# Narrower first weight loads, another order of k, q and v, and one attention block a group later, in a fused retention and gated feed-forward kernel

## The chip, the cores and the metric

The kernel runs on one core of a Trainium2 chip. The metric is the device time in microseconds (us) of one execution. A core has a matrix engine (PE, with its weight loads listed as PEld), a vector engine (DVE), a scalar engine for activations and copies (ACT), a general engine (POOL) and a synchronisation engine (SP). POOL, SP and ACT also issue transfers to the 16 DMA engines of the core. Each engine runs its own list of instructions in order; semaphores let one list wait for another. The matrix engine writes to PSUM, of which this kernel has eight banks: one reserved for the state sums (`z`) and seven that are handed round for everything else (they all carry the name `ff` in the profile).

## The reference

Two stages follow each other: a recurrent linear attention with a decay per head, and a feed-forward layer with a sigmoid gate.

```python
# q, k, v: (4 batches, 8 heads, 768 tokens, 64); gamma[h] = 1 - 2 ** (-5 - h)
for t in range(S):
    state = gamma * state + einsum('bhd,bhe->bhde', k[:, :, t], v[:, :, t])
    y[:, :, t] = 1 / sqrt(D) * einsum('bhd,bhde->bhe', q[:, :, t], state)
x = y.transpose(0, 2, 1, 3).reshape(3072, 512)
gate = 1 / (1 + exp(-(x @ w_gate)))         # w_gate, w_val: 512 x 1536
out = (gate * (x @ w_val)) @ w_out          # w_out: 1536 x 512
```

## The kernel before

**Attention.** The 768 tokens of each batch are cut into six chunks of 128, numbered 0 to 23 over the four batches. Within a chunk the recurrence becomes matrix products: scores of k and q (`scores`), a causal mask on DVE (`masks`), masked scores times v (`intra`), and q times the state that the earlier chunks left (`inter`). The decay is folded into v (`scale_v`, table `tabv`) and taken out again in the output (`y_out`, tables `taby`). `state` makes a chunk's share of the state, `state_sum` adds it up on DVE, `casts` turns the sum on ACT into a bf16 block matrix `zbd` for the next chunk's `inter`. `block(done, new)` does all this for two finished and two new chunks in one go: `inter` of the done, `scores` of the new, `intra` of the done, `state` of the new, then the vector work. Chunks 0 to 3 take a special path at the start (`..._run`). The transposes of k and q are made by the matrix engine for chunks 4 to 7 (`step_t`) and by DMA transposes that SP issues from chunk 8 on (`xbar`, line 169).

**Feed-forward.** The 3072 tokens are six tiles of 512 (four chunks each). `up(t, n1)` makes one row block of 128 of the 1536 hidden features: four matmuls with `wg`, four with `wv`, a sigmoid on ACT (`gs`), a product on DVE (`hT`). `up_columns` does several row blocks for 256 tokens in one pair of banks. `down` makes the output with `wo`, ACT copies it out and SP stores it.

**Order.** Everything is written out by hand. In the loop over the tiles `t` each `up` and each half of a `down` is a group; `plan[t]` (lines 536 to 548) names the attention steps that follow group `i`, and `ahead` (lines 557 to 563) the transfers that go before it. In tile 1 groups 0 to 7 are `up(1, 0..7)` for the first 256 tokens, groups 8 to 11 are the `up_columns` of the other 256, groups from 12 on are full `up`s. So `(4, block, 6, 8)` puts the block that ends chunks 6, 7 and starts 8, 9 behind `up(1, 4)`.

**Loads.** All loads that change type, and nearly all others, are issued by POOL in the order in which they are written: `load_run` for k, q, v of the first chunks, `load_gate_val(s)` for 256 columns of `wg` and `wv` (lines 83 to 87), `load_out` for `wo`, `load_chunk` for k, q and v of one chunk. A load takes one of eight semaphores in turn, so POOL waits before each load until the one eight loads earlier has landed. `load_behind(10)` waits for the transposes of chunk 8 before it loads chunks 10 and 11.

Of the kernel before, what the change touches and what calls it, by code (L numbers as in the profile page):

```python
# [17 lines left out]
def kernel(  # L18
# [10 lines left out]
    nc = tc.nc  # L29
# [29 lines left out]
    def load_v(g):  # L59
        vf[g] = ld.tile([C, H, D], F32, tag="vf", name="vf", bufs=6)  # L60
        nc.gpsimd.dma_start(out=vf[g], in_=src(v, g))  # L61

    def load_kq(g):
        kn[g] = ld.tile([C, H, D], BF16, tag="kn", name="kn")
        qn[g] = ld.tile([C, H, D], BF16, tag="qn", name="qn")
        nc.gpsimd.dma_start(out=kn[g], in_=src(k, g))  # L66
        nc.gpsimd.dma_start(out=qn[g], in_=src(q, g))  # L67

    def load_chunk(g):
        load_kq(g)  # L70
        load_v(g)
# [8 lines left out]
    wv = wpool.tile([128, KT, D_FF], BF16, name="wv")  # L80
    wo = wpool.tile([128, NFF, D_MODEL], BF16, name="wo")

    def load_gate_val(s):
        cols = slice(s * 256, (s + 1) * 256)
        for dst, w in ((wg, moe_w_gate), (wv, moe_w_val)):
            nc.gpsimd.dma_start(out=dst[:, :, cols],
                                in_=w.rearrange("(kk p) n -> p kk n", p=128)[:, :, cols])

    def load_out(s):
        nc.gpsimd.dma_start(out=wo[:, s * 3:(s + 1) * 3, :],  # L90
                            in_=moe_w_out.rearrange("(n p) d -> p n d", p=128)[:, s * 3:(s + 1) * 3, :])
# [60 lines left out]
    def bank(shape, dt=F32):  # L152
        return pf.tile(shape, dt, tag="ff", name="ff")
# [85 lines left out]
    def x_cols(t, kk, lo, hi):  # L239
        if hi - lo == 512:  # L240
            return xT[t][:, :, kk, :]
        half = lo // 256
        return xT[t][:, half, kk, lo - half * 256:hi - half * 256]
# [11 lines left out]
    def runs(t):  # L255
        return t.rearrange("x h (j d) -> x h j d", j=2)
# [19 lines left out]
    def scale_run(a, eng):  # L276
        vsr[a] = const.tile([128, H, 2, D], BF16, name=f"vsr{a}")
        eng.tensor_tensor(vsr[a], runs(vr[a]), tabr[:, a].unsqueeze(3).to_broadcast([128, H, 2, D]), op=ALU.mult)  # L278
# [20 lines left out]
    def inter_run(g, first=True):  # L299
        a, c = divmod(g, 2)  # L300
        if first:
            y[g] = bank([128, NP, C])
        if g > 0:
            for p in range(NP):
                nc.tensor.matmul(y[g][:, p, :], zbd[g - 1][:, p, :], qT[a][:, p, :, c * D:(c + 1) * D],
                                 start=(first and p == 0), stop=not first, skip_group_check=True)
# [72 lines left out]
    def up(t, n1, lo=0, hi=512, between=None):  # L379
        if t not in hT:  # L380
            hT[t] = ffn.tile([128, NFF, 512], BF16, tag="hT", name="hT", bufs=2)
        ps = []
        for w in (wg, wv):
            u = bank([128, 512])
            for kk in range(KT):
                nc.tensor.matmul(u[:, lo:hi], w[:, kk, n1 * 128:(n1 + 1) * 128], x_cols(t, kk, lo, hi),  # L386
                                 start=(kk == 0), stop=(kk == KT - 1))
            ps.append(u)
        if between:
            between()  # L390
        gs = ffn.tile([128, 512], F32, tag="gs", name="gs")
        nc.scalar.activation(gs[:, lo:hi], ps[0][:, lo:hi], AX.Sigmoid)  # L392
        nc.vector.tensor_tensor(hT[t][:, n1, lo:hi], gs[:, lo:hi], ps[1][:, lo:hi], op=ALU.mult)  # L393

    def up_columns(t, n1s, lo, hi, rows=1):
        if t not in hT:
            hT[t] = ffn.tile([128, NFF, 512], BF16, tag="hT", name="hT", bufs=2)
        n = hi - lo
        us = [bank([128, 512]), bank([128, 512])]
        for row in range(rows):  # L400
            for w, u in zip((wg, wv), us):
                for i, n1 in enumerate(n1s):
                    for kk in range(row * KT // rows, (row + 1) * KT // rows):
                        nc.tensor.matmul(u[:, i * n:(i + 1) * n], w[:, kk, n1 * 128:(n1 + 1) * 128],  # L404
                                         x_cols(t, kk, lo, hi), start=(kk == 0 and (rows == 1 or i == 0)),
                                         stop=(kk == KT - 1), skip_group_check=rows > 1)
        ps = [u[:, :len(n1s) * n] for u in us]
        gs = ffn.tile([128, 512], F32, tag="gs", name="gs")
        g = gs[:, :len(n1s) * n]
        nc.scalar.activation(g, ps[0], AX.Sigmoid)  # L410
        nc.vector.tensor_tensor(hT[t][:, n1s[0]:n1s[-1] + 1, lo:hi], g.rearrange("p (i n) -> p i n", n=n),  # L411
                                ps[1].rearrange("p (i n) -> p i n", n=n), op=ALU.mult)
# [18 lines left out]
    def keep_on(n, u):  # L431
        for _ in range(n):
            nc.tensor.matmul(u, ident, ident4, start=True, stop=True)  # L433
# [24 lines left out]
    for i in range(2):  # L458
        half = maskr[i * D:(i + 1) * D]
        nc.gpsimd.affine_select(half, half, pattern=[[-1, 2], [1, 2], [2, D]], base=0, channel_multiplier=-2,  # L460
                                compare_op=ALU.is_ge, fill=0.0)
    maskr2 = maskr.rearrange("x j i p -> x (j i p)").unsqueeze(1).to_broadcast([128, 2, 4 * D])
    load_gate_val(0)
    load_gate_val(1)
    load_gate_val(2)
    scale_run(1, nc.gpsimd)
    warm = bank([128, 4, 128])
    keep_on(9, warm)
    kT[0], qT[0], kT[1], qT[1] = (new_run_T() for _ in range(4))
# [22 lines left out]
    masks_run(1, 0)  # L492
    masks_run(1, 1)
    keep_on(2, warm)
    up_columns(0, range(0, 2), 0, 256)
    inter_run(2)
    state_run(1)
    sum_run(2)
# [11 lines left out]
    extend_taby(5)  # L510
    for s in range(4):
        load_out(s)
    for g in range(4, 8):
        load_chunk(g)
    y[3] = bank([128, NP, C])
    intra_run(1, [3])
    y_out_run(2)
# [15 lines left out]
    def downs(t):  # L533
# [2 lines left out]
    plan = {  # L536
        0: [(9, step_t, 4), (10, step_t, 5), (11, block, None, 4), (12, step_t, 6), (13, casts, 4), (13, step_t, 7),
            (14, block, 4, 6), (15, scale_v, 8)],
        1: [(0, casts, 6), (2, scale_v, 9), (4, block, 6, 8), (6, casts, 8), (10, scale_v, 10), (11, scale_v, 11),
            (12, block, 8, 10), (14, casts, 10), (16, scale_v, 12), (17, scale_v, 13), (20, block, 10, 12),  # L540
            (22, casts, 12)],
        2: [(3, scale_v, 14), (4, scale_v, 15), (6, block, 12, 14), (8, casts, 14), (11, scale_v, 16),
# [69 lines left out]
```

## Time and profile before

| what | value |
|---|---|
| median of 4 runs | 231.28 us (230.95 to 231.86) |
| the profiled execution: its time, its span | 231.15 us, 229.4 us |
| PE, PEld busy | 219.3 us (96%), 119.0 us (52%) |
| DVE, ACT, POOL busy | 117.8 us, 87.1 us, 78.5 us |
| mean granted clock of PE | 0.998 |
| POOL's DMA queue (q0) | 55440 packets, 16.78 MB |
| one 256-column load of `wg` or `wv` | 256 KB as written, 7.2 or 7.8 us from issue to landing (median) |

The span is the stretch from the first to the last instruction that the profiler recorded. The profiled execution's own time has 1.75 us more than its span. Sizes of loads and rates in GB/s count the bytes that are written: a load that turns f32 into bf16 reads twice as much.

### The profile page before, as it was taken

To read this page: it belongs to the slowest core of one execution; us is meant where nothing else is said; L and a number is where in the kernel's file an instruction comes from. 1 tells how busy PE (TensorE), PEld (TensorE's weight loads), DVE (VectorE), ACT (ScalarE), POOL (GpSimd) and SP (SyncE) were. 2 spreads that over 40 slices of the span, in tenths; PEclk is the share of its full clock that TensorE was granted. 3 is DMA by queue.
4 is the path that set the end of the run, shared out by engine and by line. 5 is a ranking of instruction groups with operands and counts; after the bars stand their busy time and mean duration, and the time that the engine had idled before them with its cause. 6 is when DMAs were issued, how large, how long until landed. Compare 5 with 4: busy or idle time off the path is not lost.

```text
span 229.4 us, 4519 instructions
## 1 busy us (share of the span) xinstructions
PE 219.3 (96%) x1803; PEld 119.0 (52%) x1815; DVE 117.8 (51%) x224; ACT 87.1 (38%) x162; POOL 78.5 (34%) x106
## 2 busy tenths in 40 slices
PE   4989999999799999999999999999999999999994
PEld 1458544567687445445445445455445454444443
DVE  5687333459776927367626267637267520243301
ACT  5785332554362421632521532622432512433221
POOL 7899956840906353081630090620000000000000
PEclk9999999999999999999999999999999999999999
DMA  8999999999996999499892399892410012100022
GB/s 135 217 196 197 198 206 195 180 245 202 154 173 36 176 137 228 120 127 162 61 202 96 91 130 138 90 197 83 108 39 3 0 49 91 46 0 0 4 91 91
DMA packets 77653, 28.08 MB, mean 122 GB/s; under 512 B 64192, under 2 KB 73280, under 8 KB 77632
## 3 DMA queue, kind: packets, MB, share of 16 engines
q0 software_dynamic: 55440, 16.78, 66.0%
q1 hardware_dynamic: 22048, 10.95, 22.9%
q8 instruction: 14, 0.23, 0.4%
q10 hardware_dynamic: 144, 0.07, 0.1%
q14 instruction: 7, 0.06, 0.1%
HBM read 28.31 MB, written 6.29 MB: 151 GB/s over the span
## 4 chain that ended last, share of the span: by engine, by line
PE 84%; DMA 10%; POOL 2%; issue 1%; DVE 1%; SPq 1%; DVEq 0%
PE ff L386 47%; PE ff L422 23%; PE ff L404 5%; DMA kn<-in_k_dram 4%; DMA wv<-in_moe_w_val_dram 3%; PE ff L232 2%; DMA qkX<-qn 2%; DMA vr<-in_v_dram 2%; PE ff L183 2%; PE ff L195 1%; PE ff L441 1%; PE z L201 1%; DVE vsr L278 1%; SPq L169 1%; PE ff L162 0%
## 5 line engine op out<-in xcount | busy, mean ns | idle before, releaser
L393 DVE TENSOR_TENSOR hT<-gs,ff 128x512 bf16<-128x512 f32 (+1 forms) x70 | 44.7, 647 | 59.2 <-PE ff L386 53.4
L386 PE MATMUL ff<-xT,wg 128*128 128x512 bf16 (+1 forms) x280 | 67.7, 364 | 0.2 <-DVE hT L393 0.2
L386 PE MATMUL ff<-xT,wv 128*128 128x512 bf16 (+1 forms) x280 | 67.6, 364 | 0.1
L392 ACT ACTIVATE gs<-ff 128x512 f32<-128x512 f32 (+1 forms) x70 | 39.4, 567 | 68.2 <-PE ff L386 62.2
L422 PE MATMUL ff<-wo,hT 128*128 128x512 bf16 x264 | 61.1, 379 | 0.9 <-issue 0.5
L386 PEld LDWEIGHTS <-wv 128*128 128x128 bf16 x280 | 27.3, 98 | 29.3 <-DMA wv<-in_moe_w_val_dram 0.3
L422 PEld LDWEIGHTS <-hT 128*128 128x128 bf16 x276 | 26.4, 98 | 30.5
L386 PEld LDWEIGHTS <-wg 128*128 128x128 bf16 x280 | 26.8, 98 | 28.3 <-issue 0.4
L427 ACT COPY ob<-ff 128x512 f32<-128x512 f32 x23 | 13.5, 585 | 49.1 <-PE ff L422 39.0
L250 DVE TENSOR_TENSOR xT<-ff,taby 128x512 bf16<-128x512 f32 x20 | 12.9, 685 | 24.0 <-PE ff L232 24.0
L553 POOL COPY gate<-qkX 1x1 bf16<-1x1 bf16 x7 | 1.2, 177 | 58.7 <-DMA qkX<-qn 58.7
L66 POOL DMA_DIRECT2D kn<-in_k_dram x20 | 17.8, 892 | 7.7 <-DMA qkX<-kn 2.9
L207 ACT CAST zbd<-za 64x256 bf16<-64x256 f32 x38 | 15.3, 403 | 10.0 <-DVE za L219 4.8
L61 POOL DMA_DIRECT2D vf<-in_v_dram x20 | 18.3, 917 | 1.6 <-DMA wo<-in_moe_w_out_dram 1.0
L67 POOL DMA_DIRECT2D qn<-in_q_dram x20 | 18.0, 898 | 2.0 <-DMA wo<-in_moe_w_out_dram 1.6
L174 DVE TENSOR_TENSOR vs<-vf,tabv 128x512 bf16<-128x512 f32 x20 | 13.5, 685 | 5.6 <-DMA vf<-in_v_dram 5.6
L188 DVE TENSOR_TENSOR stA<-ff,causal 128x512 bf16<-128x512 f32 x20 | 13.6, 679 | 0.0
L189 DVE TENSOR_TENSOR stB<-ff,causal 128x512 bf16<-128x512 f32 x20 | 13.6, 679 | 0.0
L433 PE MATMUL ff<-ident 128*128 128x512 bf16 x15 | 5.8, 527 | 3.0 <-POOL ident masks.py:199 3.0
L404 PE MATMUL ff<-xT,wg 128*128 128x256 bf16 x56 | 7.3, 273 | 0.7 <-DMA wg<-in_moe_w_gate_dram 0.7
L404 PE MATMUL ff<-xT,wv 128*128 128x256 bf16 x56 | 7.3, 273 | 0.3 <-DMA wv<-in_moe_w_val_dram 0.3
L411 DVE TENSOR_TENSOR hT<-gs,ff 128x512 bf16<-128x512 f32 x7 | 4.7, 687 | 3.9 <-PE ff L404 3.8
(86 smaller groups left out, 150.1 us busy)
## 6 DMA issues: line engine op xcount, KB each, us to landing
out_dram<-ob SPq DMA_DIRECT2D x23, 256.0 KB, 2.2
vf<-in_v_dram POOLq DMA_DIRECT2D x20, 256.0 KB, 5.7
kn<-in_k_dram POOLq DMA_DIRECT2D x20, 128.0 KB, 5.5
qn<-in_q_dram POOLq DMA_DIRECT2D x20, 128.0 KB, 5.7
wg<-in_moe_w_gate_dram POOLq DMA_DIRECT2D x6, 256.0 KB, 7.2
wv<-in_moe_w_val_dram POOLq DMA_DIRECT2D x6, 256.0 KB, 7.8
wo<-in_moe_w_out_dram POOLq DMA_DIRECT2D x4, 384.0 KB, 9.6
vr<-in_v_dram SPq DMA_DIRECT2D x1, 512.0 KB, 4.4
```

The lines of the kernel that those rows point to most:

```text
L61: nc.gpsimd.dma_start(out=vf[g], in_=src(v, g))
L66: nc.gpsimd.dma_start(out=kn[g], in_=src(k, g))
L67: nc.gpsimd.dma_start(out=qn[g], in_=src(q, g))
L174: nc.vector.tensor_tensor(vs[g], vf[g], tabv[:, g % NCH, :].unsqueeze(2).to_broadcast([C, H, D]), op=ALU.mult)
L188: nc.vector.tensor_tensor(stA[g], sc[g][0], causal4, op=ALU.mult)
L189: nc.vector.tensor_tensor(stB[g], sc[g][1], causal4, op=ALU.mult)
L207: nc.scalar.copy(zbd[g % 4][half, :, half], z[half])
L386: nc.tensor.matmul(u[:, lo:hi], w[:, kk, n1 * 128:(n1 + 1) * 128], x_cols(t, kk, lo, hi), start=(kk == 0), stop=(kk == KT - 1))
L392: nc.scalar.activation(gs[:, lo:hi], ps[0][:, lo:hi], AX.Sigmoid)
L393: nc.vector.tensor_tensor(hT[t][:, n1, lo:hi], gs[:, lo:hi], ps[1][:, lo:hi], op=ALU.mult)
L404: nc.tensor.matmul(u[:, i * n:(i + 1) * n], w[:, kk, n1 * 128:(n1 + 1) * 128], x_cols(t, kk, lo, hi), start=(kk == 0 and (rows == 1 or i = ...
L422: nc.tensor.matmul(o, hT[t][:, n1, sm * 128:(sm + 1) * 128], wo[:, n1, :], start=(n1 == 0), stop=(n1 == NFF - 1))
```

## The change

1. `load_gate_val` gets a width. The first 256 columns of `wg` and `wv` are loaded in four pieces of 128 columns (gate 0, value 0, gate 1, value 1) in place of two of 256. The work on the first 256 tokens of tile 0 follows the pieces: `up(0, 0)` and `up(0, 1)` in place of one `up_columns` for both row blocks. POOL's `scale_run(1)` keeps six loads before it; the loads of the third block of columns come behind it.
2. Chunks 6 and 7: k and q of both are loaded first, then v of both.
3. In tile 1 `block(6, 8)` comes behind group 5 in place of 4; `casts(6)` behind group 2 in place of 0, `scale_v(9)` behind 3 in place of 2, `casts(8)` behind 9 in place of 6.

```diff
-    def load_gate_val(s):
-        cols = slice(s * 256, (s + 1) * 256)
+    def load_gate_val(s, width=256):
+        cols = slice(s * width, (s + 1) * width)
...
-    load_gate_val(0)
+    load_gate_val(0, 128)
+    load_gate_val(1, 128)
     load_gate_val(1)
+    scale_run(1, nc.gpsimd)
     load_gate_val(2)
-    scale_run(1, nc.gpsimd)
...
-    up_columns(0, range(0, 2), 0, 256)
+    up(0, 0, 0, 256)
+    up(0, 1, 0, 256)
...
-    for g in range(4, 8):
-        load_chunk(g)
+    load_chunk(4)
+    load_chunk(5)
+    for load in (load_kq, load_v):
+        load(6)
+        load(7)
...
-        1: [(0, casts, 6), (2, scale_v, 9), (4, block, 6, 8), (6, casts, 8), (10, scale_v, 10), (11, scale_v, 11),
+        1: [(2, casts, 6), (3, scale_v, 9), (5, block, 6, 8), (9, casts, 8), (10, scale_v, 10), (11, scale_v, 11),
```

## The prediction

> **What bounds the kernel now.** I read the page's busy rows first, then the list of whom PE waits for, then the chain around the longest of these waits, then PE's and ACT's timeline there, and last the rates of the load queue by stretch.
>
> ```profile
> span 229.4 us, 4519 instructions
> PE 219.3 (96%) x1803; PEld 119.0 (52%) x1815; DVE 117.8 (51%) x224; ACT 87.1 (38%) x162; POOL 78.5 (34%) x106
> DMA  8999999999996999499892399892410012100022
> ```
> ```profile
> PE ff L183 <- DMA qkX<-qn: 1.1, 1, 1.1
> PE ff L404 <- DMA wg<-in_moe_w_gate_dram: 0.7, 1, 0.7
> ...
> PE ff L404 <- DMA wv<-in_moe_w_val_dram: 0.3, 1, 0.3
> PE ff L386 <- DVE hT L393: 0.2, 1, 0.2
> PE ff L162 <- DMA qn<-in_q_dram: 0.2, 1, 0.2
> ```
> ```profile
> 45.67 8.07 DMA kn<-in_k_dram
> ...
> 53.77 1.19 SPq L169
> ...
> 55.00 4.72 DMA qkX<-qn
> 59.72 0.14 issue
> 59.86 0.40 PE ff L183 x8
> ```
> ```profile
> 56.88 0.60 PE L386 MATMUL ff<-xT,wg 128*128 128x256 bf16 x4 [0.19 <-DVE hT L393]
> 57.58 0.60 PE L386 MATMUL ff<-xT,wv 128*128 128x256 bf16 x4
> 58.01 0.39 PE L195 MATMUL ff<-qkT,zbd 128*128 128x128 bf16 x4
> 58.33 0.40 PE L183 MATMUL ff<-qkX 64*128 64x128 bf16 x8
> 59.86 0.40 PE L183 MATMUL ff<-qkX 64*128 64x128 bf16 x8 [1.13 <-DMA qkX<-qn]
> ```
> ```profile
> 55.47 1.65 ACT L207 CAST zbd<-za 64x256 bf16<-64x256 f32 x4 [1.36 <-DVE za L217]
> ```
> ```profile
> 6.00:9.00 3.00, 3.00 (x70) 1.58 (x69) 1.36 (x4) 1.82 (x4) 2.24 (x6) 1.00 1.75 174
> 14.00:27.00 13.00, 11.99 (x152) 8.64 (x152) 8.30 (x15) 7.04 (x14) 12.93 (x17) 1.00 1.45 197
> ```
>
> PE is busy for 96% of the span at full clock (the 1.00 before the last two figures of the last fence's rows is the granted clock, then come DMA share and GB/s written). Past 61.0 us PE's waits are only two "issue" gaps of 0.16 us and 0.1 us for DVE at 61.9, so a change pays only through the waits of the second fence. The last of them in time, 1.13 us at 59.86, decides: there PE needs the transposed k and q of chunk 9, and by the chain this moment is set by transfers alone (k of chunk 9 issued at 45.67, landed 8.1 us later; the transpose of q issued at 55.00, landed at 59.72). The busy share of the DMA engines is 9 tenths from the first slices to about 55 us: the whole stretch is one full load queue. So whatever PE gains or loses before 58 us is swallowed by this wait, and the end of the kernel is: landing of chunk 9's transposes, plus the PE work that then remains.
>
> **The change part by part.**
>
> *The weight pieces.* In the last fence the final number of a row is GB/s written. A 256-column load (256 KB, 512 B per row) takes 262144 B / 197 GB/s = 1.33 us of the queue. No row shows a 128-column weight piece (128 KB, 256 B per row), but the first k and q loads write the same 256 B out of 512 B: 131072 B / 174 GB/s = 0.75 us (between 6 and 7 us the rate was 183 GB/s, which makes 0.72). Four pieces in place of two loads: 4 x 0.75 - 2 x 1.33 = +0.34 us; with 0.72 it is +0.22. I take 0.28. The bounds: at the wide loads' 197 GB/s the pieces cost nothing (0); if a piece took the queue as long as a wide load, +2.66. The value lies by the rows with the same piece size, at the low end.
>
> On this stage: before, PE started on the first gate columns at 14.72, the value columns at 16.04 and ended at 16.92 (0.44 us for each four matmuls). After, gate 0 can be there at about 14.1, but PE also needs `y_out_run(1)`, which ends at 14.32. Value 1 is the fourth piece and lands 4 x 0.75 - 2 x 1.33 = 0.34 later than the second load did, so PE ends at 16.04 + 0.34 + 0.44 = 16.82, 0.1 earlier. The next value columns (needed by `up(0, 2)`, 18.69 before, straight off the queue) come 0.3 later, so PE is 0.3 late from there: the 0.7 and 0.3 us waits are moved, not removed. Two sigmoids and two products in place of one each cost 2 x 0.38 - 0.60 = 0.16 us on ACT and 2 x 0.41 - 0.69 = 0.13 on DVE, both under the waits for weights. POOL issues two loads more, 2 x 0.76 = 1.5 us; `scale_run(1)` keeps its place, `extend_taby(3)` ends about 1.6 us later, at 18.0, and its reader starts at 19.6. POOL's later issues stay at least 2 us ahead of the queue, until the wait for the load eight places earlier sets their pace as before.
>
> *The order of chunks 6 and 7.* The same bytes; q of 7 comes one v load earlier (256 KB at the 233 GB/s of the stretch from 45 to 49 us, 1.1 us), which ends PE's wait at 48.28 (0.32 us with the matmuls that were held up). v of 6 lands about 2.3 us later, near 48.5; DVE scales it and v of 7 by 50.5, and the state matmuls need them at 51.4. What is late next: PE is at chunk 7's scores 0.2 us before ACT has copied its transposes. Worth 0.15 us net, in front of the wait: nothing at the end.
>
> *The block one group later.* `up(1, 5)` (0.875 us: eight matmuls between 61.01 and 61.885) moves in front of the block, that is in front of the wait, and no longer stands behind it: -0.875. For this PE has to reach chunk 9's scores before they land. In front of the block PE now loses 0.36 us at 56.88 and 0.26 at 57.58, because ACT does the casts (1.65 us) ahead of the sigmoids of groups 1 to 4. With the casts behind group 2 the sigmoids of 0 to 2 go first, banks come free in time and both gaps close (DVE's first product, held by the masks to 56.4 before and 56.6 after, frees its banks for group 5 at 57.6). PE starts tile 1 at 53.2 (53.03 before, 0.15 for chunk 7) and is at chunk 9's scores after six groups, `inter(7)` and chunk 8's scores: 53.2 + 6 x 0.875 + 2 x 0.22 = 58.9. They land at 59.72 + 0.28 = 60.0. So the wait stays, at about 1.1 us. The casts end at 57.6; `inter(7)` needs the first of them at 58.4. `scale_v(9)` ends near 59.0, its state matmuls come at 61.2. `casts(8)` now holds ACT from 66.6 to 68.25 and one sigmoid by 0.5 us, under PE work of seven banks; their reader, `block(8, 10)`, comes at 72. On SP and POOL nothing else is moved past: the transposes of chunks 10 and 11 hang on the same queue, 0.28 us later, landed at 71.0 before, needed at 73.2 before and 72.6 after.
>
> *Sum.* -0.875 + 0.28 = -0.60 us against the profiled execution's 231.15: 230.55, a span of 228.8. The median of the runs is 0.13 above that execution, so 230.68 for a median. Measurements of this kernel tell about 0.3% (0.69 us) from no change; the forecast of -0.26% lies just inside.
>
> *A rule against the trace.* The Trainium skill ("DMA: Bandwidth & Descriptors", section "Why small descriptors are slow (HBM only)") gives each packet about 3 cycles on top of one per 32 B. By it a 256 B piece takes 11 cycles and a 512 B one 19, an estimate of 0.77 us for the piece, +0.42 on the queue and -0.45 at the end, not -0.60. The same page's "Specifications" has DMA engines read before they write below 512 B, which speaks against narrow pieces; the rows at 174 to 183 GB/s against 197 show a loss of 7 to 12%.
>
> **The rivals.**
>
> *The delay does not reach chunk 9.* If the pieces move at the wide rate, or the 8.1 us that a load spends in the queue hold slack, the landing stays at 59.72 and the gain is the whole group: 231.28 - 0.875 = 230.4. For: the bytes written fall from 233 GB/s between 45 and 49 us to 221 between 50 and 54. Against: the engines' share stays at 9 tenths there.
>
> *The group is not won.* The wait grows by as much as PE is earlier, or DVE's products (DVE is busy without a gap from 51.4 to 56.8) take over as the wait behind the block: 231.3. This needs +0.875 on the queue, a piece of 0.88 us or 149 GB/s, below any row of 256 B pieces.
>
> *Slower: a piece costs the queue what a wide load costs.* A price per packet, not per byte: 512 packets either way. Then chunk 9 lands 2.66 us later and the end moves by -0.875 + 2.66 = +1.8: 233.1. It becomes slower than before from a piece of 0.88 us on, and slower by 0.3% from 1.06. For: the packet count of the four pieces is double that of the two loads, and their rows lie 6 KB apart, where k's lie together. Against: the queue passed 197 GB/s / 512 B = 385 packets of a wide load in a microsecond, but 174 GB/s / 256 B = 680 of the first k and q.
>
> **How the numbers follow.** Main case 0.58, 230.68; its own range 230.4 to 230.95 (+0.22 to +0.34 on the queue, and 0.2 for the scatter of a median); it falls to 0.24 faster, 0.34 same. No delay at chunk 9: 0.20, of which 0.18 faster, 0.02 same. Group not won: 0.08, 0.07 same and 0.01 slower. Per-packet price: 0.14, slower. Together faster 0.42, same 0.43, slower 0.15. The low end is the full group with 0.3 us of scatter below, 230.1; the high end is the case of no gain with 0.3 above, 231.6. That leaves out the per-packet case and a few hundredths.
>
> **What would show it.** Right: PE's wait for the transposed q still there and 1.0 to 1.3 us long, near 60.1; `up(1, 5)` in front of it with no gaps at group 4; the wait for gate columns below 0.4 us and a longer one for value columns at `up(0, 2)`; rates of 170 to 185 GB/s in the first 3 us of weights. Wrong: the transposes of chunk 9 landing before 59.7 or after 60.4, PE coming to them later than they land, or a new wait past 62 us.

## The result

The changed kernel takes 231.81 us (median of 44 runs, 230.97 to 234.14) where the kernel before, on the same chip, takes 231.27 (63 runs, 230.56 to 233.34): a ratio of 1.0035, 95% interval 1.0023 to 1.0047. It is slower by 0.54 us; forecast was 0.60 us less, in a range of 230.1 to 231.6. In 13 of the 44 executions the mean granted clock was 0.993; half the clock for some 3.4 us, as two traces further down show it, would make this mean. The median of the other 31 is 231.64, still +0.37. Among the later experiments one execution of `changed_third` took 384.29 us at a mean clock of 0.66 and one of `ahead_columns` 261.02 us at 0.855; the medians and ratios given for these two leave them out.

The profiled execution of the changed kernel took 231.12 us, the third fastest of the 44, and its span is that of the kernel before. So it shows why the forecast gain is missing; the 0.69 us more that the median execution took are not in it. First its page, the same rows as were shown of before:

```profile
span 229.4 us, 4525 instructions
PE 219.2 (96%) x1803; PEld 119.1 (52%) x1815; DVE 117.9 (51%) x225; ACT 87.6 (38%) x163; POOL 80.1 (35%) x108
DMA  7999999999998999999792399992420012100022
```

Then whom PE waited for, in us in total, times, longest:

```profile
PE ff L386 <- DMA wg<-in_moe_w_gate_dram: 0.6, 1, 0.6
PE ff L183 <- DMA qkX<-qn: 0.6, 1, 0.6
...
PE ff L386 <- DMA wv<-in_moe_w_val_dram: 0.5, 1, 0.5
PE ff L183 <- DVE vs L174: 0.5, 1, 0.5
```

The chain that ended last, with start and duration of each step:

```profile
46.82 8.89 DMA kn<-in_k_dram
...
55.73 1.19 SPq L169
...
56.96 3.63 DMA qkX<-qn
```

And PE's timeline around chunk 9's scores:

```profile
58.46 0.60 PE L386 MATMUL ff<-xT,wv 128*128 128x256 bf16 x4
58.90 0.39 PE L195 MATMUL ff<-qkT,zbd 128*128 128x128 bf16 x4
59.77 0.40 PE L183 MATMUL ff<-qkX 64*128 64x128 bf16 x8 [0.48 <-DVE vs L174]
60.73 0.40 PE L183 MATMUL ff<-qkX 64*128 64x128 bf16 x8 [0.56 <-DMA qkX<-qn]
```

The group did move in front of the wait: the block now stands behind six gapless groups. But the wait's end moved as well, from 59.86 to 60.73, by 0.87 us, and a group is worth 0.875. At the start of tile 1's first `up_columns` the two are level to 0.01 us, first the kernel before, then the changed one:

```profile
63.73 0.49 PE L404 MATMUL ff<-xT,wg 128*128 128x256 bf16 x3
```
```profile
63.72 0.49 PE L404 MATMUL ff<-xT,wg 128*128 128x256 bf16 x3
```

So in the profiled pair the question is why chunk 9 came 0.87 us later and not 0.28. The load queue's rates (the last figure of a row, GB/s written) point to the weights, behind the pieces rather than in them. Before wrote 197 GB/s from 14 to 27 us, and the same from 17 to 27 us:

```profile
17.00:27.00 10.00, 9.96 (x136) 7.07 (x135) 5.62 (x10) 4.47 (x10) 9.93 (x15) 1.00 1.45 197
```

The changed kernel:

```profile
6.00:9.00 3.00, 2.87 (x70) 1.58 (x69) 1.38 (x4) 1.87 (x4) 2.27 (x6) 1.00 1.76 171
...
14.00:27.00 13.00, 11.60 (x148) 8.21 (x148) 7.98 (x16) 6.91 (x14) 12.93 (x17) 1.00 1.43 186
17.00:27.00 10.00, 9.46 (x134) 7.00 (x133) 5.00 (x10) 4.19 (x10) 9.93 (x14) 1.00 1.41 188
```

In the stretch from 17 to 27 us nearly everything on the queue is wide weight loads, the same in both kernels, and yet it is slower. POOL's timeline says what else is different there, first before's issues of the third and the fourth gate load, then the changed kernel:

```profile
11.89 0.78 POOL L86 DMA_DIRECT2D wg<-in_moe_w_gate_dram  x1
...
16.32 0.81 POOL L86 DMA_DIRECT2D wg<-in_moe_w_gate_dram  x1
```
```profile
12.60 0.79 POOL L86 DMA_DIRECT2D wv<-in_moe_w_val_dram  x1
13.45 1.90 POOL L278 TENSOR_TENSOR vsr<-vr,tabr 128x1024 bf16<-128x1024 f32 x1
15.30 0.81 POOL L86 DMA_DIRECT2D wg<-in_moe_w_gate_dram  x1
16.10 0.76 POOL L86 DMA_DIRECT2D wv<-in_moe_w_val_dram  x1
16.86 1.07 POOL L146 TENSOR_TENSOR taby<-taby,gup 128x512 f32<-128x512 f32 x1
17.84 0.81 POOL L86 DMA_DIRECT2D wg<-in_moe_w_gate_dram  x1
```

The third block's gate load is issued at 15.30, before it was at 11.89 (1.90 us of `scale_run(1)` and two loads more ahead of it); the fourth block's at 17.84, before 16.32.

### The profile page after: what moved, and what is told of

The parts are those of the page before. It is cut to its first block, busy times and chain, and to the rows that moved or that the text cites. A ratio compares the mean times of both kernels' runs of the same rounds, so it can differ in the third digit from the quotient of the medians.

```text
span 229.4 us, 4525 instructions
## 1 busy us (share of the span) xinstructions
PE 219.2 (96%) x1803; PEld 119.1 (52%) x1815; DVE 117.9 (51%) x225; ACT 87.6 (38%) x163; POOL 80.1 (35%) x108
## 4 chain that ended last, share of the span: by engine, by line
PE 82%; DMA 10%; POOL 3%; issue 1%; DVE 1%; SPq 1%; DVEq 0%
PE ff L386 47%; PE ff L422 23%; PE ff L404 5%; DMA kn<-in_k_dram 4%; DMA wv<-in_moe_w_val_dram 3%; PE ff L232 2%; DMA vr<-in_v_dram 2%; PE ff L183 2%; DMA qkX<-qn 2%; PE ff L195 1%; PE ff L441 1%; POOL wg L86 1%; PE z L201 1%; POOL wv L86 1%; DVE vsr L278 1%
## 5 line engine op out<-in xcount | busy, mean ns | idle before, releaser
L393 DVE TENSOR_TENSOR hT<-gs,ff 128x512 bf16<-128x512 f32 (+1 forms) x72 | 45.4, 640 | 58.1 <-PE ff L386 53.9
L386 PE MATMUL ff<-xT,wg 128*128 128x512 bf16 (+1 forms) x288 | 68.9, 362 | 0.8 <-DMA wg<-in_moe_w_gate_dram 0.6
L386 PE MATMUL ff<-xT,wv 128*128 128x512 bf16 (+1 forms) x288 | 68.8, 361 | 0.6 <-DMA wv<-in_moe_w_val_dram 0.5
L392 ACT ACTIVATE gs<-ff 128x512 f32<-128x512 f32 (+1 forms) x72 | 40.2, 562 | 70.2 <-PE ff L386 63.9
L386 PEld LDWEIGHTS <-wv 128*128 128x128 bf16 x288 | 28.0, 98 | 30.2 <-DMA wv<-in_moe_w_val_dram 1.4
L386 PEld LDWEIGHTS <-wg 128*128 128x128 bf16 x288 | 27.5, 98 | 29.5 <-DMA wg<-in_moe_w_gate_dram 1.5
L66 POOL DMA_DIRECT2D kn<-in_k_dram x20 | 17.9, 893 | 4.8 <-DMA qkX<-kn 1.4
L61 POOL DMA_DIRECT2D vf<-in_v_dram x20 | 18.4, 919 | 1.5 <-DMA wo<-in_moe_w_out_dram 1.0
L67 POOL DMA_DIRECT2D qn<-in_q_dram x20 | 17.9, 896 | 2.5 <-DMA wo<-in_moe_w_out_dram 2.0
L207 ACT CAST zbd<-za 64x256 bf16<-64x256 f32 x38 | 15.3, 403 | 6.8 <-DVE za L219 3.1
L232 PE MATMUL ff<-stA,vs 128*64 128x128 bf16 x80 | 6.3, 222 | 0.0
L232 PE MATMUL ff<-stB,vs 128*64 128x128 bf16 x80 | 6.3, 222 | 0.0
L411 DVE TENSOR_TENSOR hT<-gs,ff 128x512 bf16<-128x512 f32 x6 | 4.1, 686 | 4.3 <-PE ff L404 3.0
```

What stands on the lines that cost most here:

```text
L207: nc.scalar.copy(zbd[g % 4][half, :, half], z[half])
L232: nc.tensor.matmul(y[g][i * D:(i + 1) * D, p, :], vs[g][:, 2 * p + i, :], st[:, p, :], start=(first and p == 0), stop=True, skip_group_che ...
```

## The experiments

Differences are medians against the kernel before on the same chip in the same series. The ratio is estimated from all the executions and not from the two medians, so the two can differ (most in `changed_third`); its interval is a 95% interval.

### Which part costs

`loads_alone`: the first part of the change (narrow pieces, two row blocks, POOL's order), without the other two.

> Only the first part: the four narrow weight pieces, the two row blocks made one after the other, and POOL's order around them; loads of chunks 6 and 7 and the plan of tile 1 as before. Theory 1 (the pieces hold up the load queue as far as chunk 9): PE's wait at chunk 9's scores is 0.7 to 0.9 us longer than before, with nothing moved in front of it: 232.0 to 232.2. Theory 2 (the order of chunks 6 and 7 holds up the loads of 8 and 9): the pieces themselves cost the queue 0.3 us as I forecast, 231.6. Theory 3 (PE's longer wait for value columns at 19 us lets its clock be throttled in some executions): a mean granted clock of 0.993 in about three of ten executions, those 1.5 to 2 us longer than the rest.

232.25 us against 231.18: +1.07, ratio 1.0046 (1.0031 to 1.0062). The first part alone loses more than the whole change.

`order_alone`: k and q of chunks 6, 7 ahead of their v, nothing else.

```diff
-    for g in range(4, 8):
-        load_chunk(g)
+    load_chunk(4)
+    load_chunk(5)
+    for load in (load_kq, load_v):
+        load(6)
+        load(7)
```

> Only the second part: k and q of chunks 6 and 7 ahead of their v. Theory 1: the same bytes in another order, PE's 0.3 us at chunk 7 lie in front of the wait for chunk 9: 231.3, no change. Theory 2: k of chunk 9 is issued about 1 us later than before (45.67) and lands 1 us later: 231.8 to 232.3. Theory 3: clock 1.00 throughout, as the start is the old one.

231.21, ratio 0.9995 (0.9981 to 1.001): no difference, as forecast.

`block_alone`: the plan of tile 1, nothing else.

```diff
-        1: [(0, casts, 6), (2, scale_v, 9), (4, block, 6, 8), (6, casts, 8), (10, scale_v, 10), (11, scale_v, 11),
+        1: [(2, casts, 6), (3, scale_v, 9), (5, block, 6, 8), (9, casts, 8), (10, scale_v, 10), (11, scale_v, 11),
```

> Only the third part: the block of chunks 6 to 8 behind group 5, the casts behind groups 2 and 9. All theories: the transposes of chunk 9 land where they did (59.7), one group of 0.875 us more lies in front of them, PE waits about as long as before, 230.4. If it is not faster, the gain was never there: then something behind the block waits in its place. Theory 3: clock 1.00.

230.22, ratio 0.9960 (0.9943 to 0.9977): -0.96. `order_and_block` makes both of these edits.

> The changed kernel without its first part: second and third alone. Theory 1: 230.4, as with the third part alone, so the first part is what eats the gain. Theory 2: 230.9 to 231.4, the order eats it. Theory 3: clock 1.00, no executions near 233.

230.26, ratio 0.9960 (0.9944 to 0.9976): -0.92. Its chunk 9, with wide weights, was there at 60.23, and PE still waited for it:

```profile
60.23 0.40 PE L183 MATMUL ff<-qkX 64*128 64x128 bf16 x8 [1.10 <-DMA qkX<-qn]
```

So the term of -0.875 for the group stands (measured -0.92 and -0.96), and the loss lies in the first part. One trace is a coarse measure of chunk 9, though: in `block_alone`, also with wide weights, PE resumed at 60.61.

### Pieces, row blocks, or the number of loads

`pieces_only`: the narrow pieces and POOL's order, with the old `up_columns`.

```diff
...
-    load_gate_val(0)
+    load_gate_val(0, 128)
+    load_gate_val(1, 128)
     load_gate_val(1)
-    load_gate_val(2)
     scale_run(1, nc.gpsimd)
+    load_gate_val(2)
```

> The four narrow weight pieces and POOL's order around them, but the two row blocks still made together by up_columns; the rest as before. Queue theory (the pieces themselves cost the load queue about 0.9 us): as with the whole first part, 232.1 to 232.3, PE's wait at chunk 9 near 2 us. Rival (the loss comes from the row blocks made one after the other, with their own banks, sigmoids and products): 231.2 to 231.4.

232.49 against 231.35: +1.14, ratio 1.0040 (1.0022 to 1.0059). The row blocks are not needed for the loss.

`rows_only`: the two row blocks with wide loads.

```diff
-    up_columns(0, range(0, 2), 0, 256)
+    up(0, 0, 0, 256)
+    up(0, 1, 0, 256)
```

> Wide loads as before, but up(0, 0) and up(0, 1) in place of up_columns. Queue theory: 231.1 to 231.4, no change, as the wait for chunk 9 swallows what PE does at 16 us. Rival (the row blocks are the loss): 232.

231.37, ratio 1.0017 (0.9992 to 1.0041). No loss by itself that can be told from none.

`half_rows`: as many loads of as many bytes as in `pieces_only`, but each with two of the four row groups at full width, so that a row is written in 512 B as before and not in 256.

```diff
+    def load_half_rows(s, half):
+        cols, kks = slice(s * 256, (s + 1) * 256), slice(half * 2, half * 2 + 2)
...
-    load_gate_val(0)
+    load_half_rows(0, 0)
+    load_half_rows(0, 1)
     load_gate_val(1)
-    load_gate_val(2)
     scale_run(1, nc.gpsimd)
+    load_gate_val(2)
```

> The same number of loads of the same size as the changed kernel's four pieces, but cut the other way: each takes two of the four row groups at the full 256 columns, so a row that is written stays 512 B; the row blocks by up_columns; the rest as before. If the price is that of narrow rows: 231.1 to 231.4, no change. If it is that of two loads more (issue, end of each load): 231.9 to 232.2.

232.41, +1.06, ratio 1.0044 (1.0028 to 1.0059). The same loss with wide rows. The narrow rows do show in the rate (12 to 15 us: 173 GB/s in `pieces_only`, 199 in `half_rows`, 191 before), but not in the loss. So a narrow piece's rate or price per packet does not explain it: what these two kernels share is two loads more and the third block behind `scale_run(1)`.

`pieces_doubled`: the first 512 columns in eight pieces of 128.

```diff
...
-    load_gate_val(0)
-    load_gate_val(1)
-    load_gate_val(2)
+    load_gate_val(0, 128)
+    load_gate_val(1, 128)
+    load_gate_val(2, 128)
     scale_run(1, nc.gpsimd)
+    load_gate_val(3, 128)
+    load_gate_val(2)
...
-    up_columns(0, range(0, 2), 0, 256)
+    up(0, 0, 0, 256)
+    up(0, 1, 0, 256)
```

> The first part alone, with the first 512 columns of both tensors in eight narrow pieces in place of four wide loads. If each narrow piece has its price on the queue, the loss of 1.07 us against before doubles: 233.1 to 233.5, and v of chunk 5, which landed at 43.25 before and 44.15 in the changed kernel, lands near 45.0. If the loss is paid once (a start that is out of step), 232.2 to 232.4.

234.82, +3.47, ratio 1.0153 (1.0128 to 1.0179): three times the loss for twice the pieces, more than either theory had. In its trace the queue runs almost dry about 17 us: between 17.0 and 17.2 us 9 packets began, against 117 to 142 in each such stretch from 18.2 to 19.4. The fourth pair of pieces had been issued at 16.0, behind `scale_run(1)`.

### Late issue

`late_third`: wide loads, nothing narrow, no load added; only the third block's two loads go behind `scale_run(1)`.

```diff
     load_gate_val(1)
-    load_gate_val(2)
     scale_run(1, nc.gpsimd)
+    load_gate_val(2)
```

> Edit: the kernel before with one move: the two loads of the third block of weight columns are issued behind POOL's scale_run(1) in place of ahead of it. Same loads, same sizes, same rows, up_columns kept. What is open: how much of the +1.07 us of the four narrow pieces is the price of the pieces themselves on the queue, and how much is that the loads behind them are issued 1.5 us later on POOL and find the queue empty. Theory 1 (late issue): the loads of the third block are issued at about 15.4 and 16.1 us in place of 11.9 to 13.4, as in the changed kernel, the queue runs dry at about 17 us, the rate of the stretch from 17 to 27 us falls from 197 GB/s to 170 to 190, the value columns of the sixth block land later than 29.4 (29.9 to 31), and the time is 0.4 to 1.2 us above before. Theory 2 (price of the pieces): queue and time as before, 231.1 to 231.5, 197 GB/s, sixth block at 29.4.

232.21 against 231.07: +1.14, ratio 1.0048 (1.0033 to 1.0064), the whole loss of `pieces_only` with not one piece. With only four loads ahead of it, `scale_run(1)` sat waiting until its v had landed at 13.88 (the profile names another release), so the third block went out at 15.90, a little later still than in the changed kernel:

```profile
14.05 1.90 POOL L278 TENSOR_TENSOR vsr<-vr,tabr 128x1024 bf16<-128x1024 f32 x1 [2.31 <-ACT qkT L269]
15.90 0.81 POOL L86 DMA_DIRECT2D wg<-in_moe_w_gate_dram  x1
```

Its rate from 17 to 27 us:

```profile
17.00:27.00 10.00, 9.98 (x138) 7.22 (x136) 6.10 (x11) 4.74 (x10) 9.92 (x14) 1.00 1.30 171
```

The profile gives the time from a load's issue to its landing. For the weight loads issued between 15 and 19.6 us, least, median and most: first before (fourth block to the first load of the sixth), then the changed kernel (third block to the first load of the fifth), then `late_third` (third and fourth block).

```profile
DMA to landing us min/median/max: 6.3/7.5/8.7
```
```profile
DMA to landing us min/median/max: 5.4/5.9/7.0
```
```profile
DMA to landing us min/median/max: 4.9/5.3/5.6
```

A load in a full queue waits for its turn, so its time to landing is long. Where it falls to about 5 us, this reads as a load that was first in line, with only the time left that it needs on an idle queue. The kernel before shows this value at its start too: the first k load, issued by POOL at 1.31 us with nothing ahead of it on that queue, landed at 6.33.

`pieces_early`: narrow pieces, and the third block ahead of `scale_run(1)`, which runs 1.3 us later for it.

```diff
...
-    load_gate_val(0)
+    load_gate_val(0, 128)
+    load_gate_val(1, 128)
     load_gate_val(1)
     load_gate_val(2)
     scale_run(1, nc.gpsimd)
```

> Edit: four narrow pieces for the first 256 columns, up_columns kept, and the loads of the third block issued ahead of scale_run(1), so that eight loads and not six stand before it (scale_run ends some 1.5 us later, near 17 us). Theory 1 (late issue): only the pieces' own price on the queue stays, some 0.3 to 0.7 us at the second block's value columns (19.0 to 19.4), nothing is added from there to the sixth block (29.7 to 30.1), 190 GB/s or more from 17 to 27 us, and the time is 0.3 to 0.6 above before, half of the 1.1 us of the pieces with the late third block. Theory 2 (price of the pieces): as with the late third block, 232.2 to 232.6 (+0.9 to +1.3). A miss of both is possible where PE then waits for scale_run near 17 us; that wait would be swallowed at chunk 9.

231.89, +0.82, ratio 1.0030 (1.0016 to 1.0045): more than expected of the pieces alone. The records show that only half of the late issue was gone, since the fourth block's loads still went out at 17.6. The table sets it beside the others; its times are those of each kernel's one trace, its last column is from the medians. A load ends in sixteen shares, one for each DMA engine; its first share is the cleaner measure of the queue, because for the third to sixth block the last engine's share comes 0.8 to 2.6 us later, differently from execution to execution, with and without the change.

| kernel | third gate load: issued, first share, apart | fourth: issued, first share, apart | sixth value load: first share | time against before |
|---|---|---|---|---|
| before | 11.9, 18.53, 6.6 | 16.3, 21.20, 4.9 | 27.89 | 0 |
| order_and_block | 11.8, 18.46, 6.7 | 16.2, 21.14, 4.9 | 27.95 | -0.92 |
| changed | 15.3, 18.96, 3.7 | 17.8, 21.66, 3.8 | 28.77 | +0.54 |
| pieces_only | 15.4, 19.02, 3.6 | 17.9, 21.75, 3.8 | 28.87 | +1.14 |
| half_rows | 15.8, 19.49, 3.7 | 18.4, 22.13, 3.8 | 29.67 | +1.06 |
| late_third | 15.9, 19.53, 3.6 | 18.4, 22.27, 3.8 | 29.41 | +1.14 |
| pieces_early | 13.2, 18.80, 5.6 | 17.6, 21.45, 3.8 | 28.44 | +0.82 |
| changed_ahead | 13.2, 18.64, 5.5 | 16.6, 21.29, 4.7 | 27.97 | -0.28 |

In this table a wide load that was issued late had its first share 3.6 to 3.8 us after the issue and not sooner; one issued in time had it at the moment the queue set. The table's sixth value load is late by 0.9 to 1.8 us in the kernels with both blocks on this floor, by 0.55 with one, and by 0.1 at most with none (28.07 is the latest of the six kernels with wide loads in time). Of the repeats below one falls out of line: in `changed_columns_2` both blocks were on the floor (3.8 and 3.9 us) and the sixth value load was 0.36 late.

The narrow pieces sat near this floor too: in the changed kernel, issued every 0.73 to 0.77 us, each of the four had its first share 3.3 to 3.5 us behind its issue, while the wide loads of before fell back from 4.3 to 6.0 us. By this measure POOL was not far enough ahead of the queue even for the pieces.

That the queue's delay reaches chunk 9 is seen over all the traces. In the seven with the sixth value load's first share at 27.89 to 28.07 chunk 9's transposed q landed at 59.3 to 60.5; in the nine with it at 28.65 to 29.67 it landed at 60.6 to 62.0. (Of the others, `pieces_early` with 28.44 landed at 60.2, `changed_columns_2` with 28.25 at 59.9, `pieces_doubled` with 31.73 at 63.9.)

`changed_ahead`, in the last row, is the changed kernel with POOL's own work put off behind the loads.

```diff
     load_gate_val(1)
-    scale_run(1, nc.gpsimd)
     load_gate_val(2)
+    scale_run(1, nc.gpsimd)
...
+    load_gate_val(3)
     extend_taby(3)
-    for s in range(3, NFF // 2):
+    for s in range(4, NFF // 2):
```

> Edit: the changed kernel with POOL's work put off behind the loads: the two loads of the third block stand ahead of scale_run(1) again, the two of the fourth ahead of extend_taby(3). So far no weight load that found the queue short of work had its first share landed sooner than 3.5 to 3.8 us after its issue began, and in the changed kernel the third and fourth blocks sit on that floor. Theory 1 (late issue is what ate the gain): the gate loads of the third and fourth block stand 4.5 us or more behind their issue, 190 GB/s or more from 17 to 27 us, sixth block's value columns by 30.0, and the time -0.875 for the group plus 0.4 to 0.6 for the four pieces on the queue: 0.2 to 0.6 below before. Theory 2 (the pieces alone ate it): as the changed kernel, 0.2 to 0.6 above before. Theory 3 (POOL's scale_run, some 1.5 us later, becomes the wait): PE waits for it near 17 us and the time is above before all the same.

230.95 against 231.23: -0.28, ratio 0.9981 (0.9958 to 1.0005), and the changed kernel on the same chip, `changed_third`:

> The changed kernel beside the two others on one chip. Theory 1 (late issue): 0.3 to 0.5 above before in the executions at full clock, and 0.6 to 1.0 above the kernel with POOL's work put off. Theory 2 (the pieces): the same as that kernel.

232.25: +1.02, ratio 1.0027 (1.0003 to 1.0051), which is +0.62. The cure takes 1.3 us off on that chip by the medians, 1.1 by the ratios. Its queue is full again, as the rate from 17 to 27 us and the times to landing of the loads issued from 15 to 19.6 us say:

```profile
17.00:27.00 10.00, 9.45 (x134) 6.98 (x133) 5.13 (x11) 4.18 (x10) 9.92 (x14) 1.00 1.45 197
```
```profile
DMA to landing us min/median/max: 6.8/6.8/7.3
```

And with a full queue the four pieces cost the queue next to nothing: the sixth value load's first share is at 27.97, within the 27.89 to 28.07 of the kernels with wide loads; the third block's first share is 0.1 us later than before's, in `pieces_early` 0.3. Its -0.28 (-0.97 to +0.12 by the interval) is still 0.64 short of the -0.92 of `order_and_block`; the queue accounts for 0.1 to 0.3 of that, and whether the rest is a cost or scatter this run does not show.

### Again, and the row blocks

`changed_again`: the changed kernel beside `late_third`.

> The changed kernel once more, beside the others of this series on one chip: what its parts alone give (+1.07, +0.03 and -0.96, in all +0.14) against the +0.54 of its first measurement. Theory 1 (the parts add up but for the throttled executions): 0.1 to 0.4 us above before, and executions with a mean granted clock below 0.995 among the slowest. Theory 2 (the parts work against each other): 0.4 to 0.7 above before, in the executions at full clock too.

231.51 against 231.07: +0.44, ratio 1.0013 (0.9985 to 1.0040). Its profiled execution (231.54 us) lost its time in another place:

```profile
18.10 0.61 PE L386 MATMUL ff<-xT,wg 128*128 128x256 bf16 x4
20.86 0.39 PE L386 MATMUL ff<-xT,wv 128*128 128x256 bf16 x2 [2.15 <-DMA wv<-in_moe_w_val_dram]
```
```profile
60.65 0.76 PE L183 MATMUL ff<-qkX 64*128 64x128 bf16 x16
```

The last share of the value columns that `up(0, 2)` needs came 3.6 us behind the first: 17.26 and 20.81. PE was so late from there that it met chunk 9 without a wait. Here the end was set by PE's own delay, not by the load of chunk 9.

`changed_columns`: the changed kernel with the one `up_columns` of before.

```diff
-    up(0, 0, 0, 256)
-    up(0, 1, 0, 256)
+    up_columns(0, range(0, 2), 0, 256)
```

> Edit: the changed kernel with the one up_columns of the kernel before for the first two row blocks. Open is whether the two row blocks one after the other make executions with a mean granted clock of 0.993 more frequent (13 of 44 of the changed kernel, 5 of 12 with wide loads and the two row blocks, none of 28 of before beside these). Theory 1 (the row blocks do): none or one of 12 executions at 0.993, and a median 0.1 to 0.3 below the changed kernel. Theory 2 (the chip does): as many as the changed kernel in this series, and the same median.

231.04 against 231.23 (-0.19, ratio 0.9988, 0.9960 to 1.0017), beside `changed_third`: 1.21 us below it, although its third and fourth block went out as late (15.25 and 17.80). By this series alone the row blocks would be as good a cause as the late issue. Both once more on one chip, `changed_columns_2` and `changed_fourth`:

> The changed kernel with up_columns, on the same chip as the next: does it stand below the changed kernel again? Theory 1 (the row blocks cost): 0.4 to 1.2 below the changed kernel. Theory 2 (scatter): within 0.3 of it, both 0.1 to 0.6 above before.

> The changed kernel beside the other two. By all three measurements so far it is 0.4 to 1.0 above before. Theory 1 (the row blocks cost) and theory 2 (scatter) differ in its distance to the kernel with up_columns: 0.4 to 1.2, or within 0.3.

231.15 (ratio 1.0003, 0.9979 to 1.0027) and 231.35 (1.0008, 0.9982 to 1.0034) against 231.27: 0.20 apart. The first distance did not come again. `ahead_columns` has both, POOL's work put off and `up_columns`.

> Edit: the changed kernel with both: the loads of the third block ahead of scale_run(1) and of the fourth ahead of extend_taby(3), and the one up_columns of the kernel before for the first two row blocks. Theory 1 (both cost, apart from each other): 0.5 to 1.2 below before, below each of the two single cures (-0.28 and -0.19). Theory 2 (only the late issue costs; the gain of up_columns was scatter): -0.2 to -0.5, as with the late issue cured alone.

230.33 against 231.27: -0.94, ratio 0.9952 (0.9926 to 0.9978). It is below both single cures, but its interval overlaps theirs. Whether the two row blocks cost something next to the moved block (0.2 to 1.2 us by three comparisons; `rows_only`, with the block in its old place, shows no cost) or only scatter stays open.

### A kernel that beats both

`block_two_later`: wide loads, chunks 6 and 7 in the new order, and the block behind group 6.

```diff
-        1: [(0, casts, 6), (2, scale_v, 9), (4, block, 6, 8), (6, casts, 8), (10, scale_v, 10), (11, scale_v, 11),
+        1: [(2, casts, 6), (3, scale_v, 9), (6, block, 6, 8), (9, casts, 8), (10, scale_v, 10), (11, scale_v, 11), (10, scale_v, 10), (11, scale_v, 11),
```

The line names `scale_v` of chunks 10 and 11 twice, so DVE also makes two products of 0.68 us a second time.

> Edit: the kernel before with chunks 6 and 7's new order of k, q and v, the plan of the changed kernel, and the block behind group 6 in place of 5; wide weight loads. With the block behind group 5, PE still waits 1.1 us for chunk 9's transposes. Theory 1 (the wait is slack that another group fills): the wait falls to 0.2 to 0.3 us, and the time to 0.7 to 0.9 below that kernel, 229.3 to 229.6. Theory 2 (what stands behind the block takes over: DVE's masks and the loads of chunks 10 and 11, which start a group later): 229.9 to 230.3, no gain over the block behind group 5, and a new wait past 62 us.

229.79 against 231.07: -1.28, ratio 0.9940 (0.9926 to 0.9954), the fastest of all here; it falls short of the expected 229.3 to 229.6, with a gain of 0.36 over `order_and_block` in place of 0.7 to 0.9. The wait at chunk 9 is gone from the list; what PE waits for lies in the first 16 us, and none of it is for the products that DVE makes twice:

```profile
PE ff L433 <- POOL ident masks.py:199: 3.0, 1, 3.0
PE ff L404 <- DMA wg<-in_moe_w_gate_dram: 1.4, 1, 1.4
PE ff L266 <- DVE stB L295: 0.3, 1, 0.3
PE ff L315 <- DVE stB L295: 0.2, 1, 0.2
```

With the wait at chunk 9 gone, the wait for weights (1.4 us here, 0.9 in `order_and_block`) has none behind it that would swallow it; whether this is what the gain falls short by was not tried.

## Why the prediction was wrong

The frame was right for the profiled pair: the end is chunk 9's landing plus the PE work behind it, and the prediction's own sign of being wrong, a landing after 60.4, is there (60.59). The term that failed is the queue's, +0.28. It priced the four pieces and put the later issue of the loads behind them at nothing; the step under it is the sentence "POOL's later issues stay at least 2 us ahead of the queue". I had moved the third block's loads to behind `scale_run(1)` and compared their issue with the moment when the queue would want them, without asking how long a load takes from its issue to its first bytes. The queue wanted the third block's first share at 18.5 to 18.8 (18.53 before, 18.80 in `pieces_early`) and the fourth's at 21.2 to 21.3 (`changed_ahead`). Issued at 15.30 and 17.84, with the 3.6 to 3.8 us that the runs show, they could not come before 18.9 and 21.4; they came at 18.96 and 21.66, 0.43 and 0.46 us later than before's. By the fifth gate load (24.77, before 23.89) the delay was 0.88, and so it stayed to the sixth value load; how it doubled there is open (see the second dip in the last section). What shows the step's price is `late_third`, +1.14 with the late third block alone (issued 4.0 us later there, 3.4 in the changed kernel), and `changed_ahead`, which undoes it and takes 1.1 to 1.3 us off the changed kernel beside it.

That chunk 9 was 0.87 late in the profiled pair is not this 0.88 handed on unchanged. The first share of chunk 9's k was 0.35 later than before's (52.04 and 51.69), its last 1.96 (55.71 and 53.75), so q's transpose was issued 1.96 later, and it took 3.63 us in place of 4.72. The last share and the transpose differ from execution to execution, so that these two numbers agree is luck.

The prediction had a number at hand that should have warned: the first k load of before took 5 us from issue to landing on an idle queue, and no weight load of before less than 5.7.

| step of the prediction | forecast | measured |
|---|---|---|
| group moved in front of the wait | -0.875 | -0.92, -0.96 (`order_and_block`, `block_alone`) |
| four pieces against two loads on the queue | +0.28 (0 to 2.66) | 0.1 to 0.3 with a full queue (`changed_ahead`, `pieces_early`) |
| POOL's later issues | 0 | +1.14 in time with wide loads (`late_third`) |
| landing of chunk 9's transposes | 59.72 to 60.0 | 60.59 (before 59.72); PE resumes at 60.73 |
| order of chunks 6, 7 | 0 | 231.21 against 231.18 |
| gate columns | PE can start after 14.32 | 14.67, wait 0.64 |
| value columns of `up(0, 2)` | 18.69 to 19.0 | 19.42, wait 0.52 |
| gaps at group 4 close | yes | yes, six groups without a gap |
| PE at chunk 9's scores | 58.9, wait about 1.1 | 60.17, wait 0.56 |
| `extend_taby(3)` ends | 18.0 | 17.93 |

Of the smaller misses, the gate columns first: the piece's first share was there at 12.40, its last only at 14.62, where the whole wide load had landed at 14.68. That lag is no property of the piece: in `changed_third` and `changed_columns` it had landed at 13.3, and there PE started at 15.24 and 14.82 all the same, after a wait of 0.5 us for DVE's `xT`. So an earlier gate piece was worth nothing there. PE was later at chunk 9's scores than forecast because tile 1 started at 53.66 and not 53.2, because `inter(7)` and chunk 8's scores take 0.72 us by before's own rows (58.01 to 58.73) and not 2 x 0.22, and because chunk 8's scores waited 0.48 us for DVE, which had `scale_v(9)` from 58.95 to 59.64; the prediction had put its end near 59.0 and looked only at who reads its result. The wait for chunk 9 behind it swallowed this one. ACT's casts went where they were expected to:

```profile
56.51 1.66 ACT L207 CAST zbd<-za 64x256 bf16<-64x256 f32 x4
```

The rule of the Trainium skill that was weighed ("DMA: Bandwidth & Descriptors", section "Why small descriptors are slow (HBM only)") gave an estimate of +0.42 on the queue for the pieces. The runs show 0.1 to 0.3, and a row width of 256 or 512 B made no difference in time (`pieces_only` +1.14, `half_rows` +1.06).

Of the rivals, "the group is not won" is what the profiled execution shows: chunk 9 came 0.87 later, against the group's 0.875. Its outcome came true there, but not by its mechanism, a piece of 0.88 us. The per-packet rival fell with `half_rows` and `changed_ahead`.

The corrected sum: -0.92 for block and order and +1.07 for the whole first part (`loads_alone`), together +0.15. Of the first part the late third block alone makes as much (+1.14), so the pieces' 0.1 to 0.3 can't be added to it. Measured were +0.54, +0.44, +1.02 and +0.08 in four series: the parts do not add up exactly, and the missing few tenths are not explained. With the late issue cured the sum would be -0.92 and 0.1 to 0.3, -0.6 to -0.8, near the forecast -0.60; `changed_ahead` (-0.28, interval -0.97 to +0.12) and `ahead_columns` (-0.94, -1.71 to -0.51) both allow it and don't prove it. The scatter between series is larger than in the kernel before. What was shown of it: PE's slack at chunk 9 is 0.56 us in place of 1.13, so a delay ahead of 59 us that the old wait would have swallowed reaches the end, as in `changed_again`. What was not settled: why 13 of the 44 executions of the first series had a mean clock of 0.993, when in three later series it was 1 of 12, none and 1 of 12; `rows_only` had 5 of 12 where before had none of 28 beside it, `loads_alone` with the same row blocks none of 12.

## What to carry to other kernels

A load queue that looks full stays full only if the issuing engine is far enough ahead: compare the issue of each load with the moment when the queue reaches it, and demand the shortest time from issue to landing that the trace shows on an idle queue (here 5 us), not just "earlier". When loads are split on an engine that also computes, count what the extra issues push back, and put that engine's own work behind the loads where its readers allow it. A gain made in front of one wait is worth only what the wait's own end doesn't give back, so price the end of the wait first.

## What the runs showed of the hardware

A wide load that found POOL's queue short of work had its first share done 3.5 to 4.1 us after its issue began and landed after 4.6 to 6.0 us; a 128 KB piece had its first share at 2.8 to 2.9 us (`pieces_doubled`). In `late_third` the packets that began in 0.2 us fell from about 80 to 30 at 17.8 us and rose again from 18.2 us on, 2.3 us after the issue at 15.90. The Trainium skill ("DMA: Bandwidth & Descriptors", section "Anatomy of one DMA — SWDGE (gpsimd) path") fits such a transfer with 2.0 us and 436 bytes per ns, an estimate of 2.6 us for 256 KB, and names about 1 us to the first byte in "Specifications"; the runs show about twice either for these loads, which turn f32 into bf16.

A second dip between 22.5 and 24.5 us, in the kernels with the third and fourth block late, isn't explained by this floor: the fifth block's gate load had been issued 5.2 to 5.7 us before its first share. In the changed kernel the rate from 22 to 25 us was 181 GB/s, before 198.

```profile
22.00:25.00 3.00, 3.00 (x28) 2.56 (x27) 0.77 (x2) 1.22 (x3) 2.92 (x6) 1.00 1.37 181
```
```profile
22.00:25.00 3.00, 3.00 (x25) 2.21 (x24) 1.38 (x2) 0.78 (x3) 3.00 (x5) 1.00 1.45 198
```

Half a clock costs by where it falls. In `order_alone`'s profiled execution the clock was 0.5 from 12.5 us on for 3.4 us (the figure behind POOL's, 0.57 as a mean over the stretch), and the execution took 231.19 us, no more than the others: PE came late to chunk 9 and did not have to wait there. In `late_third`'s such a stretch came at 62.1, behind the wait, and that execution took 234.78, 2.6 us above the median of its others; 3.4 us at half the clock account for 1.7 us of that.

```profile
12.00:16.00 4.00, 3.54 (x82) 2.78 (x83) 1.38 (x3) 3.54 (x8) 3.26 (x4) 0.57 1.40 191
```
```profile
62.00:65.60 3.60, 3.56 (x49) 2.88 (x50) 2.37 (x4) 0.38 (x1) 3.21 (x4) 0.53 1.68 164
```
